# Attention with a routed expert layer: scores a step ahead of PV, loads on one queue, the tail of a batch spread over the next, clears on GpSimd, overflow blocks in threes

## The chip, the cores and the metric

The kernel runs on one core of a Trainium2 chip. The metric is the device time of one execution in microseconds; the median of several runs is given with their spread. Profiles come from one profiled execution each.

A core has TensorE (PE; its weight loads are shown as PEld), VectorE (DVE), ScalarE (ACT), GpSimd (POOL) and SyncE (SP), each with an instruction queue of its own that it works through in order, and 16 DMA engines that all queues share. Results of TensorE land in PSUM; the other data lie in SBUF.

## The reference

Eight batches of eight heads, 576 tokens, 64 columns a head. Every token attends to a window of 32 tokens on either side and to 8 global tokens, and the global tokens attend to everything; the rest is masked. The 4608 output rows of 512 columns then go through a layer of eight experts, of which each token takes one.

```python
scores = scale * np.matmul(q, k.transpose(0, 1, 3, 2))
mask = np.abs(pos[:, None] - pos[None, :]) <= window
mask = mask | is_global[:, None] | is_global[None, :]
attn = softmax(np.where(mask, scores, -1e9))
x = np.matmul(attn, v)                      # rows of all heads side by side: 4608 x 512
logits = x @ w_gate                         # 512 x 8
expert_idx = argmax(logits); gate_w = max of softmax(logits)
for e in range(8):
    xe = x[expert_idx == e]
    out[expert_idx == e] = gate_w * (np.maximum(xe @ w1[e], 0) @ w2[e])   # 512 -> 1024 -> 512
```

## The kernel before

**Attention.** The work of a batch `b` is cut into `NT` = 6 steps `t`; a step takes 48 keys of each half of the sequence, all eight heads, plus the 8 global keys. For each step `scores` (line 377) multiplies mask and keys with queries into the PSUM tile `sc`, `exps` (line 401) lets ACT write their exponentials to one of three buffers `eb`, `pvs` (line 405) multiplies them with V into the PSUM tile `pv`, and `zs` (line 419) makes the row sums in `z`. `sc`, `pv` and `z` have one buffer each. `merge_x` and `merge_z` (lines 431 to 455) add the PSUM tiles to the running sums `xt` and `zt` in SBUF, three instructions on ACT (line 444) and three on DVE (line 447 or 449), which take turns.

q and k of the next batch are cast to fp16 by GpSimd (`cast_qk`, line 282), then transposed by TensorE, one pair of heads a step in steps 1 to 4 (`trans_qk`, line 286), and copied out of PSUM by ACT (k, line 298) and DVE (q, line 295). These transposes, and everything of the tail that passes through PSUM, share the two buffers of the pool `trp` (tag `tr`).

**The tail of a batch** (class `Tail`, line 477) runs one batch later, spread by hand over the six steps (lines 674 to 699): `gate(i)` multiplies the sums with the gate weights, `logits(i)` transposes and normalizes, `route1` finds the expert of each token, `ranks` and `route2` give each token a slot in the expert's list, `rows(i, f)` transposes and normalizes the output rows, `scatter` writes them to `xslot` in HBM by six indirect DMAs on GpSimd. `join` (line 457) adds the overlap of the two halves on GpSimd, `sum_globals` (line 464) reduces the rows of the global tokens on DVE.

The order is written out by hand under `manual_schedule`: in a step come PV, merge, z, merge, the k transposes, the scores and exp of the next step, a part of the tail, the q transposes, another part of the tail. The loads of k and half of V stand on SP's queue, those of q and the other half of V on ACT's. During batches 1 to 4 two pieces of expert weights are loaded, and cast by ACT in steps 3 and 4 of the same batch.

**Experts.** For each of the eight experts (line 905) four blocks of 128 rows are gathered from `xslot` (`gather`, line 765: DVE clears the two columns of row index and gate, GpSimd issues an indirect DMA), transposed, multiplied by w1 (line 914), passed through relu by ACT and DVE in turn, multiplied by w2 (line 934), scaled and scattered to `out` (`yout`, line 794). Row buffers `xr`: eight, so that an expert's rows take the buffers of the expert before the last; output buffers `y`: four. Weights come as four pieces of 1 MB (`wfetch`), through two staging buffers, and are cast by GpSimd, DVE, DVE and ACT (lines 920 and 937).

**Overflow.** What an expert has beyond 512 rows is done in blocks of 128 rows (`ov_block`, line 945), one after another in groups of three under a run-time condition (`chain`, line 977). Here nine blocks run. Their output DMAs, unlike those of the dense experts, are ordered one after another (`free=False`).

## Time and profile before

| | us |
|---|---|
| median of 3 runs | 579.2 (573.31 to 581.93) |
| the profiled execution | 578.62 |
| its span, first to last instruction | 576.8 |
| TensorE matmul busy | 405.5 (70% of the span) |
| VectorE busy | 291.5 (51%) |
| GpSimd busy | 223.8 (39%) |
| ScalarE busy | 179.6 (31%) |
| mean granted TensorE clock, of full speed | 0.876 |

Busy time is an average over stages with different limits, so the stages are read one by one. In a timeline row the first number is the start in us from the span's start, the second the duration; then come engine, line, operation, output and inputs with their sizes, and in brackets how long the engine had stood idle before, and what ended this.

### The profile page before, as it was taken

How to read it: one execution, taken by the hardware profiler on the slowest of the kernel's cores; microseconds unless marked ns; L12 is line 12 of the kernel's file. 1: busy time of each engine (PE TensorE's matmuls, PEld its weight loads, DVE VectorE, ACT ScalarE, POOL GpSimd, SP SyncE). 2: the span in 40 equal slices, each digit the busy share in tenths (PEclk: the TensorE clock that was granted, in tenths of full speed). 3: DMA queues.
4: the chain of work that ended last, by engine and by line, in shares of the span. 5: the costliest groups of instructions: out<-in, count | busy, mean ns of one | idle time of the engine just before them, and what ended most of it. 6: DMA issues, size and time to landing. Idle time of an engine off the chain costs nothing.

```text
span 576.8 us, 15876 instructions
## 1 busy us (share of the span) xinstructions
PE 405.5 (70%) x6583; PEld 244.5 (42%) x6583; DVE 291.5 (51%) x779; ACT 179.6 (31%) x318; POOL 223.8 (39%) x279
## 2 busy tenths in 40 slices
PE   0368578695896868869785529657876968997772
PEld 0246356463664645646552314223332423443331
DVE  4353246677356675766667535374261653432321
ACT  0415347254362544434340002303303313212220
POOL 6740500806308154180405444506355557522111
PEclk9997979799777996978997659878978889999997
DMA  8896894948738575440101155665967755210000
GB/s 208 145 197 122 163 239 109 238 123 210 226 97 194 171 182 117 115 81 10 29 17 43 41 186 199 219 211 177 317 231 260 267 205 209 75 74 36 28 24 33
DMA packets 75340, 84.04 MB, mean 146 GB/s; under 512 B 44412, under 2 KB 57484, under 8 KB 75264
## 3 DMA queue, kind: packets, MB, share of 16 engines
q1 hardware_dynamic: 39984, 49.43, 30.7%
q10 hardware_dynamic: 26400, 14.18, 11.1%
q0 software_dynamic: 8880, 19.37, 10.1%
q8 instruction: 54, 0.88, 0.7%
q14 instruction: 22, 0.18, 0.1%
HBM read 68.10 MB, written 16.16 MB: 146 GB/s over the span
## 4 chain that ended last, share of the span: by engine, by line
PE 25%; DVE 24%; issue 18%; DMA 18%; ACT 8%; POOL 5%; ACTq 0%; POOLq 0%; DVEq 0%
PE pv L414 8%; DMA out_dram<-y,xr 7%; DMA out_dram<-y,xo 4%; ACT xt L444 3%; DMA wall<-in_v_dram 3%; DVE xt L449 3%; DMA wall<-in_q_dram 3%; PE z L426 3%; PE h L914 2%; POOL out_dram L801 2%; ACT wall L403 2%; DVE wall L537 2%; DMA xr<-xslot_scr,idx 2%; PE tr_l L500 2%; PE tr_x L536 2%
## 5 line engine op out<-in xcount | busy, mean ns | idle before, releaser
L414 PE MATMUL pv<-wall 56*64 56x128 f32 x1536 | 64.8, 313 | 46.1 <-ACT wall L403 42.4
L914 PE MATMUL h<-xts,wall 128*128 128x512 f16 x256 | 68.9, 430 | 25.0 <-DVE ht L809 23.1
L444 ACT ACTIVATE xt<-pv 128x224 f32<-128x224 f32 x96 | 34.2, 356 | 137.2 <-PE pv L414 64.7
L414 PEld LDWEIGHTS pv<-wall 56*64 56x64 f32 x1536 | 50.6, 154 | 60.2 <-ACT wall L403 50.7
L462 POOL TENSOR_TENSOR xt<-xt 128x144 f32<-128x144 f32 x16 | 8.1, 507 | 170.4 <-DVE xt L449 170.4
L449 DVE TENSOR_TENSOR xt<-xt,pv 128x288 f32<-128x288 f32 x80 | 36.3, 454 | 72.6 <-ACT xt L444 72.6
L934 PE MATMUL yp<-wall,ht 128*128 128x512 f16 x256 | 57.6, 384 | 0.0
L914 PEld LDWEIGHTS <-wall 128*128 128x128 f16 x256 | 27.3, 107 | 63.8 <-issue 40.2
L403 ACT ACTIVATE wall<-sc 128x1024 f32<-128x1024 f32 x48 | 49.6, 1033 | 9.6 <-PE sc L396 9.4
L801 POOL DMA_INDIRECT out_dram<-y,xr x32 | 31.6, 987 | 48.0 <-DVE y L800 36.4
L811 ACT ACTIVATE ht<-h 128x512 f16<-128x512 f32 x32 | 19.1, 596 | 86.5 <-PE h L914 86.0
L280 POOL CAST wall<-wall 96x768 f16<-96x768 f32 (+1 forms) x56 | 43.6, 822 | 5.5 <-DMA wall<-in_q_dram 3.4
L536 PE MATMUL tr_x<-id,xt 128*108 128x128 f32 x192 | 33.4, 303 | 15.5 <-DVE wall L537 5.4
L768 POOL DMA_INDIRECT xr<-xslot_scr,idx x32 | 32.5, 1014 | 27.2 <-DVE xr L767 18.7
L426 PE MATMUL z<-wall,onesel 56*32 56x128 f32 x1536 | 37.9, 312 | 0.3 <-issue 0.3
L934 PEld LDWEIGHTS <-ht 128*128 128x128 f16 x256 | 25.0, 99 | 29.3 <-issue 1.4
L293 PE MATMUL tr_qk<-idh,wall 96*128 96x96 f16 x192 | 16.8, 237 | 21.3 <-ACT wall L278 21.3
L536 PEld LDWEIGHTS tr_x<-id,xt 128*108 128x108 f32 x192 | 21.5, 142 | 22.9 <-DVE wall L537 6.5
L809 DVE TENSOR_SCALAR ht<-h 128x512 f16<-128x512 f32 x32 | 21.6, 688 | 18.9 <-PE h L914 18.9
L791 PE MATMUL tx<-idh,xr 128*128 128x128 f16 x128 | 12.1, 241 | 26.9 <-DMA xr<-xslot_scr,idx 14.5
L798 ACT ACTIVATE y<-yp,xr 128x512 f32<-128x512 f32 x16 | 10.9, 684 | 63.6 <-PE yp L934 62.7
L396 PEld LDWEIGHTS <-kt 64*64 64x64 f16 x1536 | 26.5, 118 | 6.9 <-issue 2.8
(225 smaller groups left out, 714.1 us busy)
## 6 DMA issues: line engine op xcount, KB each, us to landing
st<-in_moe_w_dram SPq DMA_DIRECT2D x24, 1024.0 KB, 7.0
wall<-in_q_dram ACTq DMA_DIRECT2D x32, 288.0 KB, 5.9
wall<-in_k_dram SPq DMA_DIRECT2D x32, 288.0 KB, 9.1
wall<-in_moe_w_dram SPq DMA_DIRECT2D x8, 1024.0 KB
wall<-in_v_dram ACTq DMA_DIRECT2D x48, 96.0 KB, 5.8
wall<-in_v_dram SPq DMA_DIRECT2D x48, 96.0 KB, 5.0
wall<-vg SPq DMA_DIRECT2D x16, 96.0 KB
xr<-xslot_scr,idx POOLq DMA_INDIRECT x32, 2.8
```

Source lines behind the costliest of these rows:

```text
L280: eng.tensor_copy(o, i_)
L396: nc.tensor.matmul(out=o[:, NG:WE].rearrange("p (r a) -> p r a", r=R) if part == 0 else o[:, 0:NG], lhsT=kt[b % 2][rr, c, sl, :], rhs=rhs, ...
L403: nc.scalar.activation(out=e.rearrange("p r c w -> p r (c w)"), in_=sc[:, :, 0 : 4 * WE], func=AF.Exp, scale=0.125)
L414: nc.tensor.matmul(out=pv[64 * r : 64 * r + 64, f, c * WE : (c + 1) * WE], lhsT=vt[ff, t, 64 * h : 64 * h + 64], rhs=e[ff, r, c, :], start ...
L426: nc.tensor.matmul(out=z[32 * c : 32 * c + 32, f, 0:WE], lhsT=onesel[ff, r, :], rhs=e[ff, r, c, :], start=(r == 0), stop=(r == 1))
L444: nc.scalar.activation(out=new[i][0], in_=new[i][1], func=AF.Copy)
L449: nc.vector.tensor_tensor(out=d_, in0=d_, in1=s_, op=ALU.add)
L536: nc.tensor.transpose(out=ps[p, 128 * c : 128 * c + 128], in_=src, identity=id32)
L768: d_ = nc.gpsimd.indirect_dma_start(out=xr.bitcast(I16), out_offset=None, in_=xslot, in_offset=IndirectOffsetOnAxis(ap=ix, axis=0), bounds ...
L801: d_ = nc.gpsimd.indirect_dma_start(out=out, out_offset=IndirectOffsetOnAxis(ap=xr[:, DM : DM + 2].bitcast(I32), axis=0), in_=y, in_offset ...
L914: nc.tensor.matmul(out=ps, lhsT=w1v[:, e, c, 128 * fb : 128 * fb + 128], rhs=xts[:, c, :], start=(c == 0), stop=(c == 3))
L934: nc.tensor.matmul(out=ps, lhsT=ht[:, fc, 128 * j : 128 * j + 128], rhs=w2v[:, e, fc, :], start=(fc == 0), stop=(fc == 7))
```

## The change

- **Order in a step.** The k transposes, then scores and exp of the next step, now come first, then PV and z of this step with their merges. `eb` has two buffers instead of three; the mask moves into the space of the weights.
- **Loads.** All loads of q, k, V and gate weights are issued by SP; q is loaded together with k, right behind the casts that free the buffers. The clear of 32 unused partitions of `qf` becomes a load of as many bytes on ACT's queue.
- **Tail.** Its parts are spread differently over the steps; `sum_globals` becomes eight additions on GpSimd, behind `join`; the copy of the token numbers (line 607) moves from DVE to ACT. In the tail of the last batch `ranks` and `route2` come earlier, and its `join` is on DVE.
- **Early weights.** They are cast a batch after they are loaded, in halves, in steps 0 to 2.
- **Experts.** The clears in `gather` are on GpSimd; ten row buffers instead of eight, three output buffers instead of four.
- **Overflow.** The three blocks of a group are interleaved by hand, with a tile of its own for the transposed h, one half of which ACT copies.

```diff
-    def load_qk(b, which="kq"):
+    def load_qk(b):
         for i in range(4):
-            for w, dst, src, eng in (("k", kf, k, nc.sync), ("q", qf[32:128], q, nc.scalar)):
-                if w in which:
-                    eng.dma_start(
...
+            for dst, src in ((kf, k), (qf[32:128], q)):
+                nc.sync.dma_start(
...
-                (nc.scalar if f else nc.sync).dma_start(
+                nc.sync.dma_start(
...
+    nc.scalar.dma_start(out=qf[0:32].rearrange("p (h n) -> p h n", h=H),
+                        in_=q[0, :, 0:192].rearrange("h (p r) d -> p h (r d)", r=6))
...
-    nc.vector.memset(qf[0:32], 0.0)
...
-        for f in range(2):
-            nc.vector.tensor_reduce(out=gsum[:, f, 0:4], in_=x[:, f, :, 0, 12:XP].rearrange("p c (t g) -> p c g t", t=NT),
-                                    op=ALU.add, axis=AX.X)
-            nc.vector.tensor_reduce(out=gsum[:, f, 4], in_=z[:, f, 0, 12:XP].rearrange("p (t g) -> p g t", t=NT),
-                                    op=ALU.add, axis=AX.X)
-        nc.vector.tensor_tensor(out=xtg[:, :, s_], in0=gsum[:, 0], in1=gsum[:, 1], op=ALU.add)
+        for y, g, d in ((x[:, :, :, 0, 12:XP], gsum[:, 0:4], xtg[:, 0:4]), (z[:, :, 0, 12:XP], gsum[:, 4], xtg[:, 4])):
+            nc.gpsimd.tensor_tensor(out=g, in0=y[:, 0], in1=y[:, 1], op=ALU.add)
+            for i, (n, m) in enumerate(((0, 24), (0, 8), (0, 16))):
+                w = 24 if i == 0 else 8
+                o = g[..., 0:w] if i < 2 else d[..., 8 * b : 8 * b + 8]
+                nc.gpsimd.tensor_tensor(out=o, in0=g[..., 0:w], in1=g[..., m : m + w], op=ALU.add)
...
-            nc.vector.tensor_copy(self.x16[p, 0:J, DM:ROW].bitcast(I32)[:, :, 0],
-                                  tokg if self.glob else tokt[:, b, :])
+            nc.scalar.activation(out=self.x16[p, 0:J, DM:ROW].bitcast(I32)[:, :, 0],
+                                 in_=tokg if self.glob else tokt[:, b, :], func=AF.Copy)
...
             if b + 2 < B:
-                load_qk(b + 2, "k")
+                load_qk(b + 2)
...
+            if tr is not None:
+                trans_qk(b + 1, tr, "k")
+            if n + 1 < NT * B:
+                sc = scores(*divmod(n + 1, NT))
+                exps(n + 1, sc)
             pv = pvs(b, t)
             merge_x(b, t, pv)
             z = zs(b, t)
             merge_z(b, t, z)
-            if tr is not None:
-                trans_qk(b + 1, tr, "k")
-            if n + 1 < NT * B:
-                nb, nt = divmod(n + 1, NT)
-                sc = scores(nb, nt)
-                exps(n + 1, sc)
             if tail is not None:
-                if t == 1:
+                if t == 0:
+                    tail.gate(0)
+                elif t == 1:
                     tail.logits(0)
                 elif t == 2:
-                    tail.logits(1)
+                    tail.logits(2)
                 elif t == 3:
-                    tail.logits(2)
+                    tail.rows(0, 1)
                 elif t == 4:
+                    tail.ranks()
                     tail.rows(1, 0)
-                    tail.ranks()
-                elif t == 5:
-                    tail.rows(2, 0)
+                else:
+                    tail.rows(1, 1)
             if tr is not None:
                 trans_qk(b + 1, tr, "q")
             if tail is not None:
-                if t < 3:
-                    tail.gate(t)
+                if t == 0:
+                    tail.gate(1)
+                    tail.gate(2)
+                elif t == 1:
+                    tail.logits(1)
+                elif t == 2:
+                    tail.rows(0, 0)
                 elif t == 3:
                     tail.route1()
-                    tail.rows(0, 0)
-                    tail.rows(0, 1)
-                elif t == 4:
-                    tail.rows(1, 1)
-                else:
+                elif t == 5:
                     tail.route2()
+                    tail.rows(2, 0)
                     tail.rows(2, 1)
-            if t == 4 and b + 2 < B:
-                load_qk(b + 2, "q")
-            if wl and t in (3, 4):
-                wcast(*wl[t - 3], stage[t - 3], nc.scalar)
+            for _ in range(2 if t == 0 else 1):
+                if casts:
+                    p_, st_, hf = casts.pop(0)
+                    wcast(*p_, st_, nc.scalar, hf)
+            if t == 2:
+                for i, p_ in enumerate(staged):
+                    wload(*p_, stage[i])
+        join(b, nc.gpsimd if b + 1 < B else nc.vector)
         sum_globals(b)
-        join(b)
...
-    fy = ctx.enter_context(tc.tile_pool(name="fy", bufs=4))
-    fxr = ctx.enter_context(tc.tile_pool(name="fxr", bufs=8))
+    fy = ctx.enter_context(tc.tile_pool(name="fy", bufs=3))
+    fxr = ctx.enter_context(tc.tile_pool(name="fxr", bufs=10))
...
-        nc.vector.memset(xr[:, DM : DM + 2].bitcast(I32), 10 ** 6)
+        nc.gpsimd.memset(xr[:, DM : DM + 2].bitcast(I32), 10 ** 6)
...
+    class Block:
+        def __init__(self, i):
...
+        def x(self):
...
+        def h(self):
...
+        def t(self):
...
+                if hf:
+                    nc.scalar.activation(out=self.ht[:, 4 * hf : 4 * hf + 4, :], in_=ps, func=AF.Copy)
+                else:
+                    nc.vector.tensor_copy(self.ht[:, 4 * hf : 4 * hf + 4, :], ps)
+        def y(self):
...
-            for k_ in range(i, m):
-                ov_block(k_)
+            with tc.manual_schedule():
+                bl = [Block(k_) for k_ in range(i, m)]
+                n = len(bl)
+                bl[0].x()
+                for k_ in range(n):
+                    bl[k_].h()
+                    if k_ + 1 < n:
+                        bl[k_ + 1].x()
+                    if k_ > 0:
+                        bl[k_ - 1].t()
+                    if k_ > 1:
+                        bl[k_ - 2].y()
+                bl[n - 1].t()
+                if n > 1:
+                    bl[n - 2].y()
+                bl[n - 1].y()
             chain(m)
```

In the text, x, h, t and y with a number are these four parts of a block of the group: the transposes of its rows, the product with w1 and its relu, the transposes of h, the product with w2 and its output.

## Rows read from the trace of the kernel before

**Rows 1.** Windows by stage: start:end, length, busy us per engine (instructions), clock, DMA share, GB/s

```profile
33.12:64.72 31.60, 23.20 (x648) 17.29 (x649) 12.73 (x31) 13.31 (x28) 6.30 (x10) 0.84 0.74 142
64.72:280.76 216.04, 163.94 (x4255) 117.66 (x4255) 131.91 (x348) 95.40 (x182) 78.91 (x111) 0.87 0.61 147
280.76:343.99 63.23, 35.33 (x719) 23.24 (x719) 38.07 (x142) 10.66 (x26) 24.73 (x31) 0.74 0.22 71
343.99:514.65 170.66, 133.06 (x628) 60.61 (x628) 77.23 (x164) 40.74 (x54) 84.16 (x77) 0.90 0.59 204
514.65:576.80 62.15, 41.96 (x248) 20.18 (x247) 16.42 (x35) 11.56 (x18) 9.72 (x10) 0.94 0.10 37
```

**Rows 2.** Timeline of TensorE, batch 5, steps 1 to 3: the PV products

```profile
218.51 1.99 PE L414 MATMUL pv<-wall 56*64 56x128 f32 x32 [5.29 <-ACT wall L403]
225.36 1.10 PE L414 MATMUL pv<-wall 56*64 56x128 f32 x32
229.70 1.10 PE L414 MATMUL pv<-wall 56*64 56x128 f32 x32
```

**Rows 3.** Timeline at the change from batch 5 to batch 6

```profile
243.04 4.95 ACTq L162 DMA_DIRECT2D wall<-in_v_dram  x6
246.02 2.80 DVE L607 COPY wall<-tokt 108x6 int32<-108x6 int32 x1
248.92 0.69 DVE L537 TENSOR_TENSOR wall<-tr_x,rz 108x512 f16<-108x512 f32 x1
```

**Rows 4.** Timeline of the fourth expert and the start of the fifth

```profile
411.56 4.48 PE L914 MATMUL h<-xts,wall 128*128 128x512 f16 x20
421.62 5.17 PE L914 MATMUL h<-xts,wall 128*128 128x512 f16 x12 [5.58 <-DVE ht L809]
423.07 1.90 POOL L637 CAST wall<-st 128x2048 f16<-128x2048 f32 x1
435.36 4.48 PE L914 MATMUL h<-xts,wall 128*128 128x512 f16 x20
```

**Rows 5.** Waits: engine, line, waited for: us in total, times, longest

```profile
DVE xr L767 <- DMA out_dram<-y,xr: 48.7, 22, 5.9
```

**Rows 6.** Timeline of TensorE, second overflow block

```profile
519.54 0.39 PE L791 MATMUL tx<-idh,xo 128*128 128x128 f16 x4
520.54 1.89 PE L958 MATMUL oph<-wall,oxt 128*128 x8 [0.61 <-DVE oxt L792]
```

**Rows 7.** Timeline of the startup

```profile
2.10 2.62 DVE L200 MEMSET wall<- 32x3072 f32 x1 [0.58 <-issue]
7.31 7.82 SPq L162 DMA_DIRECT2D wall<-in_v_dram  x6
23.20 1.00 POOL L257 DMA_INDIRECT wall<-in_q_dram,ridx  x1 [0.30 <-issue]
```

**Rows 8.** Timeline of one step (batch 5, step 3): transposes, scores, merge, q copy

```profile
231.34 0.43 PE L293 MATMUL tr_qk<-idh,wall 96*128 96x96 f16 x6
231.70 0.41 PE L383 MATMUL sc<-mask,id 64*64 64x512 f16 x4
232.35 0.43 PE L515 MATMUL tr_lt<-id,lsb 128*108 128x128 f32 x2
232.54 0.30 DVE L449 TENSOR_TENSOR zt<-zt,z 128x144 f32<-128x144 f32 x1
233.74 0.45 DVE L295 COPY qt<-tr_qk 128x576 f16<-128x576 f16 x1
```

**Rows 9.** The page's costliest groups: the join on GpSimd

```profile
L462 POOL TENSOR_TENSOR xt<-xt 128x144 f32<-128x144 f32 x16 | 8.1, 507 | 170.4 <-DVE xt L449 170.4
```

**Rows 10.** Line 607, token copies: ns of one, least/median/most, first and last start

```profile
L607 DVE COPY wall<-tokt x4: 131/2404/2800, 102.9 to 307.9; 108x6 int32<-108x6 int32 x4
```

**Rows 11.** Windows of 1 us in batch 3, columns as in rows 1

```profile
169.00:170.00 1.00, 0.45 (x7) 0.27 (x5) 0.46 (x1) 0.72 (x2) 0.00 (x0) 1.00 1.00 323
171.00:172.00 1.00, 1.00 (x28) 0.95 (x20) 0.23 (x1) 0.25 (x1) 0.00 (x0) 0.50 0.99 313
```

More of the change, by code (lines that the diff above doesn't have):

```diff
@@ L82 @@
     vb = [carve(128, NT * DM, FP32).rearrange("p (t n) -> p t n", t=NT) for _ in range(2)]
-    eb = [carve(128, 8 * WE, FP32).rearrange("p (r c w) -> p r c w", r=2, c=4) for _ in range(3)]
+    eb = [carve(128, 8 * WE, FP32).rearrange("p (r c w) -> p r c w", r=2, c=4) for _ in range(2)]
     stage = [carve(128, 2048, FP32) for _ in range(2)]
@@ L455, in merge_z, with join @@
         merge(t, [(z[:, :, 0:WE], zt[b % 2])])
-    def join(b):
+    def join(b, eng):
         x, z = xt[b % 2], zt[b % 2]
@@ L630, in wload, with wcast @@
             nc.sync.dma_start(out=st.rearrange("p (c d) -> p c d", c=4), in_=src)
[L632 removed]
+    def wcast(e, w, hf, st, eng, part=None):
         o = 4096 * w + 2048 * hf
+        n, a = (2048, 0) if part is None else (1024, 1024 * part)
         if eng is nc.scalar:
[L635 removed]
+            nc.scalar.activation(out=wall[:, e, o + a : o + a + n], in_=st[:, a : a + n], func=AF.Copy)
         else:
[L637 removed]
+            eng.tensor_copy(wall[:, e, o + a : o + a + n], st[:, a : a + n])
     sc = scores(0, 0)
@@ L643 @@
     tail = done = None
+    staged = []
     for b in range(B):
@@ L651 @@
             if b + 2 < B:
-                load_qk(b + 2, "k")
+                load_qk(b + 2)
         if done is not None:
             done.scatter()
-        if 1 <= b <= 7 and pre:
-            wl = [pre.pop(0) for _ in range(min(2, len(pre)))]
-            for i, p_ in enumerate(wl):
-                wload(*p_, stage[i])
-        else:
-            wl = []
+        casts = []
+        for i, p_ in enumerate(staged):
+            for hf in range(2):
+                casts.append((p_, stage[i], hf))
+        staged = [pre.pop(0) for _ in range(2)] if b >= 1 and pre else []
         for t in range(NT):
@@ L716 @@
     tail.route1()
+    tail.rows(0, 0)
+    tail.ranks()
+    tail.route2()
+    tail.rows(0, 1)
     tg.gate(0)
+    tail.rows(1, 0)
     tg.logits(0)
-    tail.ranks()
     tg.route1()
-    tail.rows(0, 0)
-    tail.rows(0, 1)
-    tail.route2()
+    tail.rows(1, 1)
     tg.ranks()
     tg.route2()
-    tail.rows(1, 0)
-    tail.rows(1, 1)
     tail.rows(2, 0)
@@ L773, in gather @@
                 mybir.DependencyClass.Sync, mybir.DependencyReason.DATA), reason="slots of all tokens")
-    zr = [new_rows() for _ in range(8)]
+    zr = [new_rows() for _ in range(10)]
     for x_ in zr:
@@ new lines @@
+    class Block:
+        def __init__(self, i):
+            if i < NPRE:
+                self.xr = ovx[i]
+            else:
+                self.xr = new_rows()
+                gather(self.xr, ovi[:, i : i + 1])
+            self.ei = nc.values_load(ovei[0:1, i : i + 1], engines=[PE], min_val=0, max_val=E - 1)
+        def x(self):
+            self.xt = fp2.tile([128, 4, 512], FP16, tag="xts", name="oxt")[:, :, 0:128]
+            xtrans(self.xr, self.xt)
+        def h(self):
+            self.hs = fp2.tile([128, 8, 512], FP16, tag="ht", name="ohh").rearrange("p a b -> p (a b)")[:, 0:1024]
+            for hf in range(2):
+                ps = psh.tile([128, 512], FP32, tag="h", name="oph")
+                for c in range(4):
+                    nc.tensor.matmul(out=ps, lhsT=self.xt[:, c, :],
+                                     rhs=w1v[:, bass.ds(self.ei, 1), c, 512 * hf : 512 * hf + 512].rearrange("p o f -> p (o f)"),
+                                     start=(c == 0), stop=(c == 3))
+                relu(self.hs[:, 512 * hf : 512 * hf + 512], ps, hf)
+        def t(self):
+            self.ht = fp2.tile([128, 8, 128], FP16, tag="oht", name="oht")
+            for hf in range(2):
+                ps = pst.tile([128, 4, 128], FP16, tag="tx", name="oth")
+                for c in range(4):
+                    nc.tensor.transpose(out=ps[:, c, :], in_=self.hs[:, 512 * hf + 128 * c : 512 * hf + 128 * c + 128], identity=idh)
+                if hf:
+                    nc.scalar.activation(out=self.ht[:, 4 * hf : 4 * hf + 4, :], in_=ps, func=AF.Copy)
+                else:
+                    nc.vector.tensor_copy(self.ht[:, 4 * hf : 4 * hf + 4, :], ps)
+        def y(self):
+            ps = psy.tile([128, 512], FP32, tag="y", name="oy")
+            for fc in range(8):
+                nc.tensor.matmul(out=ps, lhsT=self.ht[:, fc, :],
+                                 rhs=w2v[:, bass.ds(self.ei, 1), fc, :].rearrange("p o d -> p (o d)"),
+                                 start=(fc == 0), stop=(fc == 7))
+            yout(ps, self.xr, "act", free=False)
```

55 lines of the change are left out of this document (11 added, 44 removed).

## The prediction

> **What bounds the kernel now.** I read the windows by stage first, cut at four events: the first PV product (33.12 us), the first PV of batch 1 (64.72), the first PV of batch 7 (280.76), and the first matmuls of the dense experts (343.99) and of the overflow blocks (514.65) [rows 1]. Six batches of attention cost 216.0 us, 36.0 each, and eight experts 170.7 us, 21.3 each. In neither stage is any engine busy all the time: TensorE is busy 76 and 78%, at a mean granted clock of 0.87 and 0.90. So the order of work sets the time, and the question is which hand-over ends last.
>
> Second, the timeline of one batch, reduced to the starts of PV [rows 2]. From PV to PV it takes 4.34 us where nothing is late (225.36 to 229.70), but 36.0 us for six steps, so 6.0 on average. The big loss is at each change of batch: TensorE stands still for 5.29 us, waiting for ACT's exp, and the matmuls behind the gap run at half clock (PV 1.99 us against 1.10).
>
> Third, what was late at the next such change [rows 3]: ACT has six V loads in its own queue, 4.95 us of issue; DVE sits 2.80 us in the token copy of line 607, then a 0.69 us row eviction, then the global sums. The exp of the next step stands behind the eviction of PV in ACT's order, and that waits for both.
>
> Fourth, the experts [rows 4, 5]: VectorE waits 48.7 us in 22 places to clear two columns of a row buffer whose output transfer hasn't landed. The relu behind the clear is then late, TensorE waits 5.58 us in the expert shown, and its next twelve matmuls take 5.17 us where twenty took 4.48. Fifth, the overflow blocks: one takes 5.89 us (from the stage's cut at 514.65 to the same product of the next block, 520.54), with TensorE waiting inside it [rows 1, 6].
>
> **Startup and batch 0.** The 2.62 us clear on DVE [rows 7] goes, and the address work behind it can start that much earlier. The twelve gathers of global rows follow it (1.00 us each and 0.30 between), the last at 23.20; I shift this chain by 2.6, so PV(0,0) moves from 33.12 to 30.5. The loads replace the clear by one transfer on ACT. All other loads stand on SyncE: 12 V loads, 8 for q and k. They are the same bytes, so I take nothing for them here. In batch 0 there is no tail. From PV to the end of the merge is 3.1 us (229.70 to 232.54 + 0.30 [rows 2, 8]); ACT's kt copy, exp and three evictions make about 3.45 a step, an estimate. Six steps are 20.7, and 2.5 is added for two steps at the low clock, as after the gap in [rows 2]. PV(1,0) comes at 30.5 + 23.2 = 53.7 instead of 64.72: **-11**.
>
> **Batches 1 to 6.** Exp now runs a step ahead, the V loads leave ACT, the sums leave DVE and the token copy goes to ACT. The gap of 5.29 us closes. But the k transposes move to the head of the step, ahead of scores and PV, and they take one of two PSUM buffers that the tail also uses. I schedule step 1 by hand from [rows 2, 8], with PV at 0. Merge ends at 3.14. The logits arithmetic is done at 4.04 (229.70 to 233.74). The q copy lasts 0.45, to 4.5, and frees the buffer that the next k transposes need. Those take 0.36 (231.34 to 231.70), scores 0.65 (to 232.35), hand-overs about 0.1. The next PV is at **5.6**, where it is 4.34 now. The tail behind the merge has become part of the path. The other steps by the same rows: step 2 is 5.6 as well; step 3 has a row eviction (0.69) where step 1 has logits, and the buffer it waits for is the row's: 4.9; step 4 has a row eviction, then q transposes, then scores, with no k: 5.0; step 5 has three row transposes of 0.65 in front of scores: 5.85; step 0 has three gates, the third behind the first one's eviction: 5.1. Sum 32.05. For a fall of the clock somewhere in the batch I add 1: **33** instead of 36.0, six times: **-18**. Bounds: TensorE's own work in a step is 1.64 for PV and z (229.70 to 231.34), 0.65 for scores and up to 2 for the rest, 24 us a batch at full clock if nothing waits, an estimate; DVE is busy 22.0 us a batch now (131.91 in six [rows 1]), and with its waits inside the merge I put its floor at 25. Above, 36.0, no gain.
>
> What the parts cost beside this, and their cover. The half casts of weights on ACT stand behind the merge and ahead of the next kt copy, whose transposes end at 4.4 to 4.9, while ACT's evictions are over before 3.1: over 1 us of cover a step, of which step 0, with two half casts, may use up all and lose some tenths. The eight sums on GpSimd are 2.4 us by estimate (the join's 144 columns take 0.51 [rows 9]); they stand, with 1.5 of join, ahead of the next batch's casts. The first k transposes of that batch come 10 us after the last PV began, so pair 0's two casts have 10 - 3.1 - 1.5 - 2.4 = 3.0 us; the copy in [rows 3] stood 2.8 behind more than one such cast. Without this cover each batch loses what is over. SyncE issues 24 transfers a batch; at the rate of its V loads in the crowded startup (7.82 for 6 [rows 7]) these are 31 us, inside 33. What waits there first is the load of q and k, for GpSimd's casts to free their buffers, and behind it stand weights and V, both wanted a batch later.
>
> The token copy shows a price of sharing: the same 108x6 copy took 131 ns at the least and 2.8 us at the most [rows 10], the long one of [rows 3] while GpSimd was casting. The Trainium skill, SBUF — State Buffer, section on SBUF's two separate sides, says that VectorE in a two-port mode or with two SBUF inputs and GpSimd lock each other out for a whole instruction, while ACT has a port of its own. The trace agrees for the copy. By that rule the sums that go to GpSimd would hold back DVE's routing at step 5 by up to 2.4 us a batch, 14 in all, and the sum would be 537. I take nothing: routing ends with 1.2 us of DVE work left before PV(b+1,0) has to be merged, and the casts stood there before.
>
> **Batch 7, tail and start of the experts** (63.2 us). Without q and k transposes a step has little to wait for: 24.5 instead of 26.4. In the last tail the slots come 3 us earlier, since ranks now stand behind one row; scatters, 1.3 apart, take most of it back. Two more buffers are cleared. **-3**, bounds 0 and -8.
>
> **Experts.** The clears go to GpSimd, and with ten row buffers only half of them find a transfer still under way. DVE is free. What is late next: GpSimd's cast of the first weight piece stands behind four output scatters and four gathers with clears, 5.2 + 5.6 us. In the row it began 11.5 after the expert's first matmul [rows 4]; I get 9.3, since the last scatters reach 3.7 into the expert. From that cast to the next expert were 12.3 us (load of the third piece, cast, eviction); with TensorE already waiting for this eviction I take 11.3. An expert is **20.6** for the five with pieces to wait for, where this row has 23.8. The first I put at 17.3, the seventh at 16 (no cast), the last at 14.3: by 0.22 a matmul (4.48 for 20) the products are 14.3 an expert. Sum 150.6 against 170.7: **-20**. Bounds: all at 15.5, -47; the waits only change engine, 0. I stay near the row's own loop. Three output buffers instead of four: ACT may wait a little, and three h buffers in PSUM cover it.
>
> **Overflow.** Three blocks in a pipeline. Product h of a block began 1.0 us after the transposes, 0.61 of that idle [rows 6], and the second half of h's transposes waits likewise. By order x0 h0 x1 h1 x2 t0 h2 ... the first and second block keep this wait (1.0 each: relu stands before the copy on DVE), the rest is covered: 16.1 for three. Now three take 17.7. That is -1.6 three times; the three outputs then queue at the end, each writing only after the one before has landed, +1.4. **-3.5**, bounds +2 and -9.
>
> **Sum.** The profiled execution took 578.62 us (span 576.8, 1.8 around it), 0.6 under the median 579.2 of three. 578.6 - 11 - 18 - 3 - 20 - 3.5 = **523**.
>
> **Rivals.**
> B, the transposes don't wait for the q copy because DVE is ahead: a batch is then 28, between DVE's 25 and my 33: 523 - 30 = 493. For it: 4.34 us steps exist. Against: the logits and q copy are in DVE's order ahead of what frees the buffer. 0.15.
> C, the waits in the experts only move from DVE to GpSimd, where the weight cast stands behind them: no gain there, 543. For it: GpSimd has 84 us busy of 170.7 and the casts are in its queue. 0.17.
> E, one queue of loads is late: a batch at 37 if the 31 us don't overlap with a wait of 6 for the casts, 547. Against: a whole batch lies between a load and its use. 0.09.
> D, the other side: TensorE's clock stays low in attention. At 169 us it was busy 0.45 of a microsecond at clock 1.00, and at 171 the clock was 0.50, with no full gap between [rows 11]. My step of 5.6 has two idle pieces, of 1.25 and 0.5. At half clock PV costs 0.9 more, scores and k transposes 1.0 more, both on the path: 7.5 a step, 11.4 more a batch: 523 - 6 + 68 = 585, and somewhat above with batches 0 and 7: 594. It decides from 4 or 5 low steps in six. Against: PV took its 1.10 at 225.36 and 229.70 [rows 2]. The Trainium skill, TensorE: Matmul & The Clock Gate, section on the clock gate, says that low is the default and that activity releases it; in the trace it came back in each batch. 0.09.
> Main, 523, own range 505 to 540: 0.50.
>
> About 2% is what a measurement here can tell from no change. Faster by more (below 567): A, B, C and most of E, 0.86; within 2%: 0.05; slower: 0.09. The range is 493 to 550: it takes in B, C and E and leaves out D and gains in both stages together.
>
> **What would show it.** Right: no idle of 5 us on TensorE at a change of batch; k transposes waiting for the q copy; PV to PV 5 to 5.6 at full clock; no DVE wait for an output transfer, and in its place DVE waiting for a weight piece; experts 2 to 5 about 20 us. Wrong: steps of 4.3 (B); GpSimd's clears waiting as long as DVE's did (C); SyncE's q/k loads landing after the casts want them (E); clock 0.5 in most steps (D).

## The result and the profile after

The changed kernel took 546.9 us in the median of four runs (544.37 to 552.78), the kernel before 578.0 beside it; the ratio is 0.947, 95% interval 0.939 to 0.956. It is faster by 31 us where I forecast 56; the range of 493 to 550 holds it, and the shortfall has to be found.

The windows of the changed kernel, cut at the five events of [rows 1] (start:end, length, busy us of PE, PEld, DVE, ACT and POOL, clock, DMA share, GB/s). The first cut is a little late: two matmuls of PV(0,0) run at 29.87, and the other thirty follow at 31.29, behind the load of `vg` (V of the global tokens).

```profile
31.29:57.88 26.59, 21.23 (x646) 15.89 (x647) 8.32 (x22) 12.62 (x27) 7.55 (x10) 0.94 0.97 220
57.88:261.74 203.86, 155.43 (x4262) 116.25 (x4255) 107.79 (x318) 97.89 (x196) 93.92 (x161) 0.90 0.65 156
261.74:318.99 57.25, 33.67 (x698) 22.48 (x689) 36.13 (x123) 11.13 (x29) 31.53 (x51) 0.70 0.26 83
318.99:487.60 168.61, 135.38 (x628) 60.50 (x628) 71.18 (x128) 40.18 (x54) 86.66 (x113) 0.91 0.61 205
487.60:547.30 59.70, 38.69 (x248) 20.11 (x247) 12.31 (x26) 16.60 (x27) 9.45 (x10) 0.92 0.10 36
```

| term | predicted | measured, from the windows |
|---|---|---|
| startup and batch 0 | -11 | -6.8 (PV(1,0) at 57.88 instead of 64.72) |
| batches 1 to 6 | -18 | -12.2 (203.9 instead of 216.0; 34.0 a batch) |
| batch 7, tail, start of the experts | -3 | -6.0 |
| experts | -20 | -2.1 |
| overflow | -3.5 | -2.4 |
| sum | -55.5 | -29.5 (span 576.8 to 547.3) |

So 18 of the 26 us that are missing lie in the experts.

**The middle batches** look as drawn by hand. One step 1 with the step after it, in the timeline of the changed kernel:

```profile
234.35 1.07 PE L414 MATMUL pv<-wall 56*64 56x128 f32 x32
238.32 0.45 DVE L295 COPY qt<-tr_qk 128x576 f16<-128x576 f16 x1
238.83 0.42 PE L293 MATMUL tr_qk<-idh,wall 96*128 96x96 f16 x6 [0.30 <-DVE qt L295]
239.17 0.41 PE L383 MATMUL sc<-wall,id 64*64 64x512 f16 x4
239.75 1.07 PE L414 MATMUL pv<-wall 56*64 56x128 f32 x32
```

The k transposes wait for the q copy, scores wait for them, and PV follows 5.40 after PV (forecast 5.6). I summed all rows of TensorE's waits in the six batches. Before, it waited some 34 us for ACT in 10 places and 14 for DVE in 32. After, it never waits for ACT, and some 43 us for DVE in 41 places. The gap of [rows 2] is gone, and the waits inside the tail have become part of the path. The largest row of each kernel (us, times, longest), before and after:

```profile
PE pv L414 <- ACT wall L403: 32.2, 6, 6.4
```

```profile
PE tr_lt L515 <- DVE tmp L523: 8.5, 6, 1.4
```

**The experts** have lost the wait of [rows 5], and three others stand in its place. The waits of the changed kernel in this stage for transfers:

```profile
DVE wall L638 <- DMA st<-in_moe_w_dram: 18.4, 6, 4.3
ACT wall L636 <- DMA st<-in_moe_w_dram: 15.4, 5, 4.7
ACT y L805 <- DMA out_dram<-y,xr: 15.1, 6, 4.3
PE tx L798 <- DMA xr<-xslot_scr,idx: 9.4, 9, 2.1
```

DVE and ACT wait for weight pieces, ACT for the transfer that still reads an output buffer, TensorE for gathered rows. The longest, the fifth, starts at 405.51, the sixth at 431.11:

```profile
409.71 0.69 ACT L805 ACTIVATE y<-yp,xr 128x512 f32<-128x512 f32 x1 [2.61 <-DMA out_dram<-y,xr]
410.67 0.97 POOL L808 DMA_INDIRECT out_dram<-y,xr  x1 [3.27 <-ACT y L805]
410.93 6.16 PE L921 MATMUL h<-xts,wall 128*128 128x512 f16 x20 [2.67 <-ACT ht L818]
418.11 1.90 POOL L638 CAST wall<-st 128x2048 f16<-128x2048 f32 x1
426.01 1.23 DVE L638 CAST wall<-st 128x2048 f16<-128x2048 f32 x1 [4.33 <-DMA st<-in_moe_w_dram]
```

ACT's last output of the expert before waits 2.61 us for a buffer, its relu is late and TensorE stops 2.67; the scatter behind it, the gathers behind the scatter and the cast on GpSimd are late, and with the cast the next weight piece. The cast begins 12.6 us after the expert's start (forecast 9.3); in the fourth expert, which [rows 4] show of the kernel before, it begins 12.0 after it.

### The profile page after: what moved, and what is told of

It reads as the page before. It is cut to its first block, busy times and chain, and to the rows that moved or that the text cites. A ratio compares the mean times of both kernels' runs of the same rounds, so it can differ in the third digit from the quotient of the medians.

```text
span 547.3 us, 15981 instructions
## 1 busy us (share of the span) xinstructions
PE 395.0 (72%) x6583; PEld 242.0 (44%) x6583; DVE 249.5 (46%) x682; ACT 187.7 (34%) x344; POOL 247.7 (45%) x383
## 5 line engine op out<-in xcount | busy, mean ns | idle before, releaser
L921 PE MATMUL h<-xts,wall 128*128 128x512 f16 x256 | 64.4, 410 | 10.3 <-ACT ht L818 9.7
L414 PE MATMUL pv<-wall 56*64 56x128 f32 x1536 | 63.5, 304 | 6.1 <-issue 5.0
L941 PE MATMUL yp<-wall,ht 128*128 128x512 f16 x256 | 63.6, 410 | 4.7 <-DVE y L807 4.7
L444 ACT ACTIVATE xt<-pv 128x224 f32<-128x224 f32 x96 | 34.2, 356 | 40.5 <-DVE xt L449 21.1
L941 PEld LDWEIGHTS <-ht 128*128 128x128 f16 x256 | 26.4, 104 | 38.0 <-issue 12.9
L775 POOL DMA_INDIRECT xr<-xslot_scr,idx x32 | 34.2, 1070 | 9.2 <-POOL xr L774 8.9
L798 PE MATMUL tx<-idh,xr 128*128 128x128 f16 x128 | 12.9, 238 | 30.4 <-DMA xr<-xslot_scr,idx 21.9
L536 PEld LDWEIGHTS tr_x<-id,xt 128*108 128x108 f32 x192 | 23.2, 150 | 24.5 <-issue 8.9
L298 ACT ACTIVATE kt<-tr_qk 128x576 f16<-128x576 f16 x32 | 20.7, 647 | 30.3 <-PE tr_qk L293 30.3
```

Source lines behind the costliest of these rows:

```text
L414: nc.tensor.matmul(out=pv[64 * r : 64 * r + 64, f, c * WE : (c + 1) * WE], lhsT=vt[ff, t, 64 * h : 64 * h + 64], rhs=e[ff, r, c, :], start ...
L444: nc.scalar.activation(out=new[i][0], in_=new[i][1], func=AF.Copy)
L536: nc.tensor.transpose(out=ps[p, 128 * c : 128 * c + 128], in_=src, identity=id32)
L775: d_ = nc.gpsimd.indirect_dma_start(out=xr.bitcast(I16), out_offset=None, in_=xslot, in_offset=IndirectOffsetOnAxis(ap=ix, axis=0), bounds ...
L921: nc.tensor.matmul(out=ps, lhsT=w1v[:, e, c, 128 * fb : 128 * fb + 128], rhs=xts[:, c, :], start=(c == 0), stop=(c == 3))
L941: nc.tensor.matmul(out=ps, lhsT=ht[:, fc, 128 * j : 128 * j + 128], rhs=w2v[:, e, fc, :], start=(fc == 0), stop=(fc == 7))
```

## The experiments

The jobs ran on three further chips, on which the kernel before took 609 to 612 us; stages are compared between kernels of one chip where there are such. Stage times are from one profile each. The experts with unchanged code took 168.6, 164.3, 171.4, 168.8 and 169.5 us in five profiles on four chips, so a difference of 2 or 3 us between single profiles means little. One of them is the changed kernel itself, run beside three of the others:

> The changed kernel itself again, as the measure for the three kernels beside it on the same chip (two chips gave 578 and 609 us for the kernel before; only runs on one chip are set against each other). Expected from its own record: 0.947 of the kernel before, experts 164 to 169 us, with waits of DVE and ACT for weight pieces of 30 to 34 us, of ACT for output transfers of 13 to 15, of TensorE for gathered rows of 9 to 12.

Measured: 0.955 of the kernel before (0.947 to 0.963), experts 171.4, the waits for pieces 22.0, ACT's for output transfers 21.5, TensorE's for rows 7.6. The stage is longer by 2.8 us than in the first profile, but the waits for pieces are 12 us less and ACT's 6 more: the same code shares its time out differently among these waits from run to run.

### Four output buffers (y4)

```diff
-    fy = ctx.enter_context(tc.tile_pool(name="fy", bufs=3))
+    fy = ctx.enter_context(tc.tile_pool(name="fy", bufs=4))
```

> The changed kernel with four buffers for the expert outputs again instead of three (two planning tiles share one space to make room); the ten row buffers, the clears on GpSimd and all else stay. In the changed kernel the eight experts took 168.6 us. Theory Y (three output buffers are the new wait): ACT waits 15.1 us in 6 places in the experts for an output transfer to land before it can write the next output, which holds back its relu, the fourth scatter and so the gathers and the weight cast on GpSimd. With four buffers that wait is gone, the experts fall to 150 to 158 and the kernel to about 530 to 537. Theory P (GpSimd's queue: clears, gathers and the weight cast behind them): the wait at ACT is cover for another, experts stay within 2 us, 545 to 549. Theory S (two staging buffers: a ring of load, cast, load, cast sets the pace): the same, 545 to 549, and the waits of DVE and ACT for weight pieces (18.4 and 15.4 us) stay or grow.

Measured: 0.944 of the kernel before (0.940 to 0.948), experts 159.7 where the same chip gave 164.3 with three buffers. ACT's wait for output transfers is gone, but TensorE waits longer for gathered rows, and DVE for weights:

```profile
DVE wall L638 <- DMA st<-in_moe_w_dram: 22.3, 8, 5.4
PE tx L798 <- DMA xr<-xslot_scr,idx: 16.4, 11, 4.2
```

By itself the buffer is worth at most about 5 of the missing 18 us: less than theory Y had, more than the other two.

### The first weight cast on ACT

```diff
-                wcast(*cast[fb // 4], nc.gpsimd if fb == 1 else nc.vector)
+                wcast(*cast[fb // 4], nc.scalar if fb == 1 else nc.vector)
```

> The changed kernel with the first weight piece of each expert cast by ACT, at the same place in the program, instead of GpSimd. GpSimd then only clears, gathers and scatters. In the changed kernel this cast began 12.6 us after the start of the fourth expert, behind scatters and gathers. Theory P: the third piece's load then starts about 8 us earlier in every expert, DVE no longer waits for it (18.4 us in 6 places), experts fall from 168.6 to 145 to 155, the kernel to 524 to 534. Theory S (the ring of two staging buffers): the ring gains too, but only until the loads themselves follow each other without a gap: 157 to 163 for the experts, 535 to 541, with waits for weight pieces still there. Theory Y (three output buffers): experts 165 to 170, 543 to 549, because ACT still waits for output transfers and has 1.9 us more to do per expert.

Measured: 0.958 (0.955 to 0.961), experts 164.7: nothing gained, and none of the three theories fits. The waits for weight pieces are gone from the waits view altogether, and the gathered rows are late instead (23.2 us of TensorE's time in 9 places). The timeline of its fourth expert shows why:

```profile
422.69 4.29 SPq L630 DMA_DIRECT2D st<-in_moe_w_dram  x2
429.70 1.03 PE L798 MATMUL tx<-idh,xr 128*128 128x128 f16 x8 [3.21 <-DMA xr<-xslot_scr,idx]
433.27 0.61 PE L798 MATMUL tx<-idh,xr 128*128 128x128 f16 x4 [2.54 <-DMA xr<-xslot_scr,idx]
433.68 9.58 PE L941 MATMUL yp<-wall,ht 128*128 128x512 f16 x32
```

Two weight loads now start at 422.69, ahead of three of the four gathers that GpSimd issues until 427.9; the DMA engines are busy 0.88 of the time from there to 433.68, the rows are late, and the output products stand behind their transposes. They then take 9.58 us for 32 (0.30 each, at a granted clock of 0.74), where [rows 4] have 0.22 at full clock.

### The clears on DVE again

```diff
-        nc.gpsimd.memset(xr[:, DM : DM + 2].bitcast(I32), 10 ** 6)
+        nc.vector.memset(xr[:, DM : DM + 2].bitcast(I32), 10 ** 6)
```

> The changed kernel with one part undone: the two columns of a row buffer are cleared by DVE again, with ten row buffers as in the change. My prediction gave the clears on GpSimd 20 us in the experts; measured were 2. If the move of the clears freed DVE and the gain was then taken by something else (Y, P or S), the experts stay between 166 and 172 here, and the kernel between 545 and 550: the clears are no longer what ends last. If the clears are worth what I forecast and the other parts cost it again, the experts come to 180 to 188, and the kernel to 560 to 567. If GpSimd's queue is the bound (P) and the clears lengthen it, the kernel is a few us faster, 540 to 544.

Measured: 0.955 (0.948 to 0.962), experts 166.0, against 164.3 with the clears on GpSimd.

```profile
DVE xr L774 <- DMA out_dram<-y,xr: 33.2, 10, 5.6
```

DVE waits 33.2 us again, and it costs 1.7, no more than profiles differ by. The wait on which I built a term of 20 us is one that the stage can bear.

### The weight loads left out

```diff
+        if once:
+            return [(e, w, hf, once[hf]) for w in range(2) for hf in range(2)]
```

> The changed kernel with the weight loads of the experts left out: only the first two pieces (2 of 24 MB) are loaded, and all 24 casts read those two; so the casts, the gathers, the products and the scatters stay, and the output is not the reference's from the third expert on. Theory S, widened by what the cast on ACT showed (the waits for pieces went, but the gathered rows then came late, 23 us of TensorE's wait, behind the loads that started earlier): weight loads in two staging buffers and the row transfers share the DMA engines, and whichever comes second is late. Without the loads, gathers land within 3 us, the waits for pieces are gone, and the eight experts fall from 164 to 169 to 130 to 142; the kernel by 25 to 35 us. Rival G (GpSimd issues the gathers too late whatever the DMA engines do: four scatters, four clears and four gathers, 5.2 + 5.6 us in front of them): experts 152 to 162, the kernel only 5 to 14 us faster, with TensorE still waiting for gathered rows.

Measured: 0.939 (0.930 to 0.948), experts 154.3, beside 171.4 with the loads. The first theory (130 to 142) falls; the rival's 152 to 162 holds. With DMA share 0.23 instead of 0.60, TensorE still waits 10.1 us in 8 places for rows: GpSimd works through four scatters, then four clears and gathers, before the last rows come, and all output products stand behind them in TensorE's order. This fits two rings, one of rows and one of weights, and the weights account for 17 of some 57 us above the 14.3 an expert of the products alone (8 x 14.3 = 114.4).

### The row transposes behind the second and third output product

```diff
-            for j in range(4):
-                xtrans(nxt[j], xtn[:, :, 128 * j : 128 * j + 128])
...
             yout(ps, rows_e[j], "act" if j % 2 else "dve")
+            if nxt is not None and j in (1, 2):
+                for i in (2 * j - 2, 2 * j - 1):
+                    xtrans(nxt[i], xtn[:, :, 128 * i : 128 * i + 128])
```

> The changed kernel with one new edit: the transposes of the next expert's rows stand behind the second and third output product of an expert (two each) instead of ahead of the first. So a gather may land 3.6 to 5.4 us later without stopping TensorE. Nothing is moved between queues. Theory S: the waits for gathered rows (9 to 12 us) go, but the ring of the weight pieces still sets the pace: experts 158 to 164, 1 to 1.5% off the kernel at most. Rival G: the gathers were what ended last, experts 148 to 156, 2 to 3% off the kernel.

Measured: 0.957 (0.948 to 0.967), experts 170.0, against 171.4, above both ranges. TensorE no longer waits for rows, and nearly all of it is given back by waits for weights, 82.6 us in 11 places instead of 22.0 in 11:

```profile
ACT wall L636 <- DMA st<-in_moe_w_dram: 44.0, 6, 9.1
DVE wall L638 <- DMA st<-in_moe_w_dram: 38.6, 5, 8.4
```

### All three together, and two of the three pairs

> The changed kernel with three edits: the transposes of the next expert's rows behind the second and third output product, four output buffers, and the first weight piece cast by ACT instead of GpSimd. Theory S: each of the edits alone moved the wait to the next late transfer (output buffers to gathers, the cast to gathers); together the ring runs nearly as fast as the bytes allow (about 6 MB an expert at the 400 GB/s of the busiest slices is 15 us): experts 142 to 152, the kernel 0.965 to 0.98 of the changed one. Rival G: the gathers stay last, experts 156 to 164, 0.985 to 1.0 of the changed one.

> The changed kernel with two of the three edits that together gave 146 us for the experts (171 without them): the transposes of the next expert's rows behind the second and third output product, and four output buffers. The weight cast stays on GpSimd. Theory R (two rings that lock into each other: rows, that is scatters, gathers, transposes, products; and weight pieces, that is load, cast, load in two staging buffers, whose first cast stands behind the rows' work on GpSimd): with the cast left on GpSimd the ring of the pieces stays late, as in the run with the spread alone, where DVE and ACT waited 83 us for pieces: experts 158 to 168, and 25 us or more of waits for pieces. Rival Y (the third output buffer was what mattered): experts 145 to 153, as with all three.

> The changed kernel with the other pair of edits: the spread transposes and the first weight piece cast by ACT; three output buffers as in the change. Theory R: both rings are open, what is left is ACT's wait for output transfers (7 to 21 us in the runs with three buffers): experts 148 to 157. Rival Y: without the fourth output buffer nothing is gained, experts 160 to 170.

Measured: all three 560.4 us, 0.911 of the kernel before (0.902 to 0.920), where the changed kernel took 586.1 beside it, 0.955 (0.947 to 0.963). So they are worth 4.4% of the changed kernel, more than theory S had. Without the cast on ACT 0.937 (0.930 to 0.945), without the fourth buffer 0.929 (0.922 to 0.935). The windows of the experts: the changed kernel on its chip, all three edits on the same, then spread with y4, and spread with the cast, on another.

```profile
357.70:529.07 171.37, 137.64 (x628) 61.38 (x628) 73.62 (x128) 40.15 (x54) 86.51 (x112) 0.89 0.60 202
```

```profile
355.18:501.37 146.19, 124.58 (x628) 57.02 (x628) 66.19 (x128) 50.92 (x60) 75.48 (x107) 0.98 0.70 237
```

```profile
358.03:511.89 153.86, 129.84 (x628) 59.04 (x628) 73.09 (x128) 41.16 (x54) 84.70 (x111) 0.93 0.66 225
```

```profile
358.00:509.57 151.57, 128.24 (x628) 58.42 (x628) 66.92 (x128) 50.51 (x60) 77.20 (x107) 0.95 0.67 228
```

| edits | experts, us | against unchanged experts on the same chip |
|---|---|---|
| y4 / cast / spread alone | 159.7 / 164.7 / 170.0 | -4.6 / +0.4 / -1.4 |
| spread with y4 / spread with cast | 153.9 / 151.6 | -15.3 / -17.6 (mean of 168.8 and 169.5) |
| all three | 146.2 | -25.2 |

Three edits worth -4.6, +0.4 and -1.4 alone are worth -25.2 together: each alone hands its gain to the next late transfer. The third pair, y4 with the cast, wasn't run, so whether the spread must be one of the edits stays open. For the pair with y4 the expected range of theory R (158 to 168) was too high: its waits for weights are still 46.8 us, but they cost less. Rival Y fails as well: without the fourth buffer 17.6 us were gained. About half of the 25.2 is TensorE's own busy time, which falls from 137.6 to 124.6 for the same 628 matmuls, at 0.98 of full clock instead of 0.89; the other half is its idle time, which falls from 33.7 to 21.6. The Trainium skill, TensorE: Matmul & The Clock Gate, section on the clock gate, says that activity releases the clock; these two windows agree.

### The k transposes behind z again

```diff
-            if tr is not None:
-                trans_qk(b + 1, tr, "k")
             if n + 1 < NT * B:
...
             merge_z(b, t, z)
+            if tr is not None:
+                trans_qk(b + 1, tr, "k")
```

> The changed kernel with one part undone: the transposes of k stand behind z again and no longer at the head of the step, ahead of scores; scores and exp stay one step ahead. My hand schedule says that k at the head waits for the q copy on DVE, behind the routing arithmetic, and that this makes steps 1 and 2 5.4 and 5.5 us long. If so, scores now wait only for the second tail matmul of the step: about 0.4 to 0.65 less in four steps, a batch at 32 instead of 34.0, the kernel at 535 to 540. Rival: DVE's own chain (merge, logits, q copy) sets the step wherever k stands, a batch stays at 33.5 to 34.5, the kernel 544 to 549. Second rival: q then waits for ACT's copy of k in the same step, and it gets slower, batch 35 to 36, kernel 552 to 559.

Measured: 0.967 (0.960 to 0.974); the experts begin at 357.67, with the other three kernels of this chip at 353.80 to 356.59. The steps that I had in mind did get shorter:

```profile
172.33 1.19 PE L414 MATMUL pv<-wall 56*64 56x128 f32 x32
177.01 1.07 PE L414 MATMUL pv<-wall 56*64 56x128 f32 x32
181.69 0.95 PE L414 MATMUL pv<-wall 56*64 56x128 f32 x10
```

4.7 instead of 5.0 and 5.4 for steps 0 and 1, yet the experts begin 1 to 4 us later: the gain is lost again, mostly in steps 4 and 5. Step 4 takes 6.0 to 8.2 us, with k at the head mostly 5.1 to 5.9. There the row transposes, and behind them q and scores, wait for ACT's copy of k:

```profile
242.26 0.65 PE L536 MATMUL tr_x<-id,xt 128*108 128x128 f32 x4 [1.22 <-ACT kt L298]
```

In the six batches TensorE waits 16.8 us in 23 places for this copy, which it does nowhere in the changed kernel; its waits for DVE fall to 16.6. So the second rival has the mechanism, and its size (1 to 2 us a batch) was too large. TensorE's waits for "issue", in which it waited for nothing that the profile shows, are longer as well (17.9 us in 40 places, 9.6 to 12.3 in the three others); no run settles why.

### Scores no longer a step ahead

```diff
-            if n + 1 < NT * B:
-                sc = scores(*divmod(n + 1, NT))
-                exps(n + 1, sc)
             pv = pvs(b, t)
...
             merge_z(b, t, z)
+            if n + 1 < NT * B:
+                sc = scores(*divmod(n + 1, NT))
+                exps(n + 1, sc)
```

> The changed kernel with one part undone: scores and exp of the next step stand behind z again, as before the change, and no longer ahead of PV; the k transposes stay at the head of the step, loads stay on SyncE, sums on GpSimd. The experts are untouched. If scores a step ahead is what closed the gap at the change of batch, the time from the first PV of batch 1 to that of batch 7 grows by 10 to 25 us against the two kernels with unchanged attention beside it, towards the 36 a batch of the kernel before. Rival: the gap was made by the V loads in ACT's queue and the sums on DVE alone, and those stay away: attention within 4 us of the unchanged one, or faster by up to 10, since scores then no longer wait for the k transposes.

Measured: 0.935 (0.928 to 0.941). Batches 1 to 6 take 216.2 us, with the changed order 235.3 and 231.6 on the same chip; the experts begin at 343.70 instead of 358.0 in both. So the first part of the change, taken back, lets the experts begin 14 us earlier. The theory had the wrong sign, and the rival, right in kind, allowed up to 10. The steps of this kernel:

```profile
237.23 1.10 PE L414 MATMUL pv<-wall 56*64 56x128 f32 x32
242.04 1.10 PE L414 MATMUL pv<-wall 56*64 56x128 f32 x32
246.66 1.10 PE L414 MATMUL pv<-wall 56*64 56x128 f32 x32
251.45 1.10 PE L414 MATMUL pv<-wall 56*64 56x128 f32 x32
```

4.6 to 4.8 from PV to PV, across a change of batch (the one at 242.04 is step 0). Scores behind z are issued before the tail's first matmuls, so they wait neither for the tail nor for the q copy: TensorE's waits for DVE in the six batches sum to 21.1 us, with the changed order to 42.2 and 42.0. And its waits for ACT are nil here as well, so the gap of [rows 2] stays closed without scores a step ahead.

### Half of the V loads on ACT again

```diff
-                nc.sync.dma_start(
+                (nc.scalar if f else nc.sync).dma_start(
                     out=d[64 * f : 64 * f + HW, t, :]
```

> The changed kernel with one part undone: half of the V loads (six of twelve a batch) are issued by ACT again at each change of batch, as before the change, where they took 4.95 us of ACT's queue. Scores stay a step ahead. If those loads made the gap of 5.29 us, each of seven changes of batch is 3 to 5 us longer, the attention 20 to 35 us. Rival: with exp a step ahead the loads stand behind an exp that is already done, and only the evictions behind them are late: 0 to 2 us a change, 0 to 12 in all. Startup and batch 0 may gain 1 to 3 us, since SyncE then issues six V loads less in the crowd.

Measured: 1.014 of the kernel before (1.007 to 1.021): all that the change had gained is gone, and whether it is slower than the kernel before is too close to call. Batches 1 to 6 take 264.0 us instead of 235.3 and 231.6, and PV(0,0) comes at 35.86 instead of 30.5 and 30.2, so the gain expected at startup was a loss. The rival's 0 to 12 us falls. A change of batch in this kernel:

```profile
235.41 6.66 ACTq L160 DMA_DIRECT2D wall<-in_v_dram  x6
242.17 1.02 ACT L403 ACTIVATE wall<-sc 128x1024 f32<-128x1024 f32 x1 [6.55 <-DMA wall<-in_v_dram]
245.37 0.95 PE L500 MATMUL tr_l<-xt,wgbd 128*32 128x216 f32 x8 [4.41 <-DVE lsb L504]
```

Six issues hold ACT for 6.66 us. That exp runs a step ahead doesn't help: the evictions of PV stand behind them as well, DVE's merge and gate arithmetic behind these, and TensorE waits 4.41 us for that. Step 0 takes 7.2 to 10.0 us, in the two kernels beside it 5.0 to 6.0; this is about 23 of the 30 us. Undone one at a time, the two parts are worth -17.3 (order, from the mean 233.5) and +30.5 (queue) in these batches. If the two simply add, that is 13 us of gain, near the 12.2 measured for the whole change on the first chip; both undone together weren't tried.

## Why the prediction was right and wrong

**Experts, the step that failed.** I wrote: "The clears go to GpSimd ... DVE is free. What is late next: GpSimd's cast of the first weight piece", and sized one loop through that cast, 9.3 + 11.3. In the fourth expert it began at 12.0 and the next expert 11.4 later, in the fifth at 12.6 and 13.0 later; the five experts that I put at 20.6 took 22.2 to 25.6. Worse, it was the wrong thing to size: with that cast taken from GpSimd nothing moved, and with the clears put back only 1.7 us did. The wait of 48.7 us in [rows 5] was the loudest, not the one that ended last. What the runs fit in its place are two rings at nearly the same pace: scatters, gathers, row transposes and products; and the loads and casts through two staging buffers, on the same DMA engines. Opening one place gave the time to the next, and two or three together gave 15 to 25 us. "ACT may wait a little" for the third output buffer was mis-sized too: 15.1 us of wait in 6 places, some 5 us of path. Rivals E (547) and C (543) came nearest in the number, but by luck: a batch took 34.0 and not E's 37, with GpSimd's casts waiting for no load, and GpSimd's clears did not wait for output transfers at all, as C had it.

**Batches 1 to 6: the schedule right, the reason wrong.** 34.0 a batch against 33, the waits where I put them; the time above it lies in two batches (37.6 and 35.5), the other four taking 32.4 to 33.2. Seven of 36 PV products ran at about half clock (1.85 to 1.99 us), and the low clock stayed as rare as I assumed, so rival D fell. B fell with the wait for the q copy. But I let three edits close the gap jointly. The runs give it to the load queue (+30.5 without it) and not to the scores: these, a step ahead, behind the k transposes and the tail, cost 17.3. What the sums and the token copy did for it wasn't tried. The row for it was in front of me: step 2 took 4.34 in [rows 2], and I priced the new one at 5.6.

**Batch 0.** PV(0,0) came at 29.87 (forecast 30.5). The batch took 28.0 us instead of 23.2, and 27 to 32 in all other runs with the changed loads. "They are the same bytes, so I take nothing for them here" is the term that failed: the bytes up to PV(1,0) are nearly the same, some 11 MB, but the DMA engines are busy 0.97 of the window instead of 0.74, and TensorE stops three times for nothing that the profile shows, in steps 2, 4 and 5. That is 5.2 us in all, where 4.8 are missing; before, batch 0 has no such stop.

```profile
41.76 1.30 PE L414 MATMUL pv<-wall 56*64 56x128 f32 x26 [2.50 <-issue]
51.33 0.66 PE L426 MATMUL z<-wall,onesel 56*32 56x128 f32 x27 [0.69 <-issue]
56.89 0.42 PE L426 MATMUL z<-wall,onesel 56*32 56x128 f32 x6 [2.00 <-issue]
```

In the trace a 16 KB packet of the instruction queue starts about 3 us before the end of each of them, which points to TensorE's own instructions coming late. Whether the crowd of loads makes them late wasn't tried.

**Batch 7 and tail** gained 6.0, within the bounds of 0 and -8. **Overflow**: three blocks take 15.5 to 15.8 (forecast 16.1), with the waits in the first transposes as drawn. The blocks gained 6.7 us up to TensorE's last product (forecast 4.8), and the last outputs, each behind the landing of the one before, gave 4.3 back (forecast 1.4); -2.4 against -3.5.

**The parts taken at nothing** held. The eight sums on GpSimd take 2.4 us a batch, as estimated. Beside them on DVE, the row evictions are not held back, and one addition of the routing (line 602) is:

```profile
93.01 0.58 POOL L468 TENSOR_TENSOR gsum<-xt 128x192 f32<-128x192 f32 x1
93.19 0.43 DVE L602 TENSOR_TENSOR si<-sl,invbig 108x6 int32<-108x6 f32 x1
93.67 0.72 POOL L472 TENSOR_TENSOR gsum<-gsum 128x96 f32<-128x96 f32 x2
94.09 1.29 DVE L537 TENSOR_TENSOR wall<-tr_x,rz 108x512 f16<-108x512 f32 x2
```

A row eviction takes 0.65 here, 0.69 in [rows 3]; the addition takes 0.43 to 0.47 in the tails of six batches, 0.17 in that of batch 6, beside a shorter sum, and 0.17 in the last, with GpSimd idle. The Trainium skill, SBUF — State Buffer, section on SBUF's two separate sides, has the two engines exclude each other for a whole instruction where DVE reads two inputs from SBUF; the six rows agree: this addition does, and it ends with GpSimd's, while the eviction reads one of its inputs from PSUM. What was wrong in the sum of 537 is the price of 2.4 us a batch: these rows show 0.3.

## What to carry to other kernels

The loudest wait in a view is not the one that ends last: where two or three late transfers keep the same pace, find every one of them before pricing the removal of one, and expect the gain only when the last is gone. DMA issues in the queue of an engine that also empties PSUM hold back everything behind them: here 6.66 us of them made a step some 4 us longer, and moving exp ahead didn't hide them. And when a wait is closed by reordering, compare the undisturbed step of the old order with the new one: here step 2 took 4.34 in the old order and 5.4 or more in the new.

## What the runs showed of the hardware that was not expected

The same changed kernel had a span of 547.3 us on one chip and 587.3 on another, and 37 of these 40 us lie between the first PV of batch 1 and the experts (57.88 to 318.99 is 261.1; 59.70 to 357.70 is 298.0). In one step of each batch from 2 on TensorE gets its matmuls in groups of five, about 0.75 us apart, though nothing that the profile shows is late. These six steps take 10.3 to 12.9 us where they take 3.1 to 6.3 on the first chip, together 40 us more. Such steps are in every profile of the three further chips, 10 to 13 us each, so the stages compared above all hold them. From the timeline of the changed kernel on that chip:

```profile
264.65 0.46 PE L414 MATMUL pv<-wall 56*64 56x128 f32 x5 [0.32 <-issue]
265.40 0.45 PE L414 MATMUL pv<-wall 56*64 56x128 f32 x5 [0.29 <-issue]
266.13 0.46 PE L414 MATMUL pv<-wall 56*64 56x128 f32 x5 [0.28 <-issue]
```

The DMA engines moved 71 GB/s in the 7 us around these rows, so a crowd of loads is not the cause there. What makes it, and why one chip did not show it, stays open; the kernel before slowed by about as much (578 to 611), which is why the ratios hardly differ. A version with the late scores and the three edits of the experts together, which these runs point to, wasn't tried.
